# First product in blocks of 512 tokens, and the second weight's right half decoded after the attention

## Chip, core and metric

The kernel runs on one NeuronCore of one Trainium2 chip. The metric is the device time of the whole program in microseconds (us). The core has five engines with their own instruction streams, each in order: PE (matrix products; weights go in through PEld beside it), DVE (elementwise work and reductions), ACT (copies with rounding, exp, Mish), POOL (elementwise work without access to PSUM) and SP (issues the DMAs here).

## The reference

```python
# q, k, v: (8 batches, 8 heads, 576 positions, 64)
scores = scale * np.matmul(q, k.transpose(0, 1, 3, 2))
thresh = np.max(scores, axis=-1, keepdims=True) - tau
scores = np.where(scores >= thresh, scores, -1000000000.0)
attn = np.exp(scores - np.max(scores, axis=-1, keepdims=True))
attn = attn / (np.sum(attn, axis=-1, keepdims=True) + 1e-09)
x = np.matmul(attn, v)      # heads side by side: 4608 tokens x 512
h = x @ w_in                # 512 x 2048
g = h * np.tanh(sp)         # sp = log(1 + exp(h)): Mish
out = g @ w_out             # 2048 x 512
```

The two weights arrive as 64-bit floating point numbers and are turned into 32-bit ones in the kernel ("decoded").

## The kernel before

**Precision.** PE works on `fp32r` operands, which keep fewer bits than a 32-bit number. So a number is split into a rounded upper part (a cast on ACT) and a remainder (a subtraction on DVE or POOL), and a product is made of three matmuls: upper by upper, upper by lower, lower by upper. `xh`, `xl` are the parts of x, `w1h`, `w1l` those of w_in; `hi`, `lo` those of the transposed weights of attention.

**Attention.** 288 tiles (32 pairs of heads, nine tiles each), counted by g, in a loop of steps. A step works on several tiles at different stages: `scores` (PE) of tile g+1 into one of two PSUM tiles `s0`, `s1`; `row_max` (DVE) of tile g, its exponentials (ACT, tile `e`) and `masked` (DVE, `p`); `normalise` of g-1 (POOL); `transposes` of g-2 (PE, `tp`, one PSUM buffer); `evacuate_hi` (ACT) and `lo_main` (DVE) of g-3, which read `tp`; and the products with the values of older tiles (`y`). Every engine runs in the order in which the step's code is written.

**First product.** Between the steps of batch b runs `gemm1` of batch b-1, a generator that yields after each matmul. `advance` draws a number of matmuls per step, from the tables `MIX`, `MIX_FIRST` and `MIX_LAST`; `DRAIN` is the number in the five steps after the last tile. `gemm1` makes, for each half of 288 tokens of the batch (`HB`) and each of the 16 blocks f of 128 rows of h, 12 matmuls into a PSUM tile (4 blocks of the model dimension by the three kinds), a copy by ACT into `hst`, and after two blocks a store to DRAM (`hd`).

**Decoding.** A piece is 128 x 256 numbers, loaded as pairs of 32-bit words. `first` scales both words (two activations on ACT), `clamp`, `shift` and `sign` run on DVE, `add` on POOL. In the attention the loop spreads these over several steps. w_in comes first. Then, every 14th step (`W2_STEP`), comes one of the 16 pieces of w_out's right half (`decode_w2`, tile `dec`), which goes back to DRAM (`w2d`). In the attention's last steps five pieces of the left half are decoded (`decode_top`) and four more loaded.

**Last stage of the first product.** The last batch's `gemm1` runs after the attention, in 32 units of 12 matmuls. Ahead of each unit stand the works that the table `todo` has for it: pieces of w_out's left half, and the operands of the second product. In this stage a PSUM tile is taken from `psh` (three buffers) where f % 5 is below 3, and from `psx` (two buffers, named `hx`) otherwise.

**Second product.** Strassen's method with seven products for each pair of 512 tokens by blocks of 256. It needs w_out's blocks a11, a12 (left half), a21, a22 (right half), and the sums s1 = a21 + a22, r21 = a11 - a21, r22 = a22 - r21, r12 = a12 - r22 (split as s4), each a tile of 8 x 256 columns that is split in an upper and a lower part. `combine` makes a sum in two halves of 1024 columns on DVE. `load_raw` reads a block of h, `mish` applies the function, `operand` splits it into four `ring` tiles of two rows each. The nine pairs run in order of tokens. A pair of 512 tokens does not match a batch of 576, so `load_h` reads from up to two half-batch tensors.

`units` hands out places for 8 x 256 tiles, `home()` places for pieces.

Of the kernel before, what the change touches and what calls it, by code (L numbers as in the profile page):

```python
# [5 lines left out]
F32 = mybir.dt.float32  # L6
# [8 lines left out]
P = 128  # L15
# [4 lines left out]
W2_STEP = 14  # L20
STAGES = ((0, 1, 1), (0, 1, 1), (0, 2, 4))
THIRD = ((),)
LAG = 2
XSPLIT = (4, 1, 2)
# [13 lines left out]
NBLK = 2 * B  # L38
TC = 256
G = 2  # L40
# [27 lines left out]
MIX = (11, 12, 6, 9, 8, 13, 12, 14, 16, 6, 16, 4, 12, 4, 15, 5, 16, 13)  # L68
MIX_FIRST = (11, 12, 6, 9, 8, 13, 6, 14, 22, 6, 16, 4, 12, 4, 15, 9, 16, 13, 7, 12, 5, 10, 8, 13, 12, 14, 16, 6, 16, 4, 12, 4, 15, 5, 16, 13)
MIX_LAST = (12, 14, 16, 6, 16, 4, 12, 4, 15, 5, 16, 13, 11, 12, 6, 9, 8, 13, 12, 14, 16, 6, 16, 4, 12, 4, 15, 5, 16, 13, 11, 12, 6, 9, 8, 13)  # L70
DRAIN = 18
# [115 lines left out]
def attention_moe(tc, q, k, v, tau, w_in, w_out, out):  # L187
# [3 lines left out]
    with ExitStack() as outer:  # L191
# [11 lines left out]
        with ExitStack() as first:  # L203
# [21 lines left out]
            with ExitStack() as att:  # L225
# [64 lines left out]

                def decode_w2(f):
                    st = home()
                    work = Decode(nc, st, None, None)
                    work.load(w_out[f * P:(f + 1) * P, WC:])

                    def last():
                        nc.sync.dma_start(w2d[:, f], fv(work.a))

                    return [(work.first, skip), *spread(work, STAGES[2]), (last,)]

# [234 lines left out]
                def split_x(g, x):  # L535
                    parts = []
                    for c in range(2):
                        xh = xpool.tile([P, HB], F32R, name="xh", bufs=12)
                        xl = xpool.tile([P, HB], F32R, name="xl", bufs=12)
                        parts.append((xh, xl))  # L540

                    def half(c):
                        xh, xl = parts[c]
                        sl = slice(c * HB, (c + 1) * HB)
                        nc.scalar.copy(xh, x[:, sl])
                        (nc.vector if g >= NT else nc.gpsimd).tensor_tensor(xl, x[:, sl], fv(xh), ALU.subtract)
# [3 lines left out]
                    return parts  # L550

                def gemm1(b, xs):

                    halves = (range(NF // 2), range(NF // 2, NF))
                    if b < B - 1:
                        order = [(c, fs) for c in range(2) for fs in halves]
                    else:
                        order = [(c, fs) for fs in halves for c in range(2)]
                    for c, fs in order:
                        for f in fs:  # L560
                            if b < B - 1 or f % 5 < 3:
                                h = psh.tile([P, 512], F32, name="h", tag="ph")
                            else:
                                h = psx.tile([P, 512], F32, name="hx")
                            half, at = divmod(f * P, DF // 2)
                            i = 0
                            for d in range(ND):
                                xh, xl = xs[d][c]
                                wh, wl = (w[:, d, at:at + P] for w in w1[half])
                                for a, m in ((wh, xh), (wh, xl), (wl, xh)):  # L570
                                    nc.tensor.matmul(h[:, :HB], a, m, start=i == 0, stop=i == 3 * ND - 1)
                                    i += 1
                                    if i < 3 * ND:
                                        yield
                            if f % 2 == 0:
                                hst = xpool.tile([P, 2, HB], F32, name="hst", bufs=3)
                            nc.scalar.copy(hst[:, f % 2], h[:, :HB])
                            if f % 2 == 1:
                                nc.sync.dma_start(hd[2 * b + c][:, f - 1:f + 1, :], hst)
                            yield  # L580
# [8 lines left out]
                weights2 = [lambda f=f: decode_w2(f) for f in range(NF)]  # L589
# [35 lines left out]
                def close_pair(g, pi):  # L625
                    b, hp = divmod(pi, NP)
                    batches.setdefault(b, []).append(split_x(g, pairs.pop(pi)["x"]))
# [17 lines left out]
                for g in range(NT + 5):  # L645
# [96 lines left out]
                    if b >= 1:  # L742
                        if step == 0:
                            stream = gemm1(b - 1, batches.pop(b - 1))
# [18 lines left out]

            def load_h(to, fs, at, end):

                start = at
                while at < end:
                    i, off = divmod(at, HB)
                    m = min(HB - off, end - at)
                    nc.sync.dma_start(to[:, :, at - start:at - start + m], hd[i][:, fs, off:off + m])  # L770
                    at += m
# [16 lines left out]
            def load_raw(blk, pair):  # L788

                fh, th = blk  # L790
                raw = units.take(F32)
                at = (2 * pair + th) * TC
                for s in halves:
                    load_h(raw[:, s], slice(8 * fh + s.start, 8 * fh + s.stop), at, at + TC)
                return raw
# [18 lines left out]
            homes = [(t, t[:, 4 * i:4 * i + 4].rearrange("p a b -> p (a b)")) for t in homes for i in range(2)]  # L814

            def fetch_piece(n, st):
                f = PIECE[n]
                work = Decode(nc, st, None, None, (r12 if f >= 8 else r11)[:, f % 8])
                work.load(w_out[f * P:(f + 1) * P, :WC])
                return work  # L820

            coming = early_pieces
            for work, f in zip(coming, PIECE[5:]):
                if f < 8:
                    work.to = r11[:, f].bitcast(U32)
            for n in range(9, 10):
                coming.append(fetch_piece(n, home()))
            for n in range(10, 14):
                coming.append(fetch_piece(n, homes[n - 10][1]))
            r21, r22, s1 = (units.take(F32) for _ in range(3))  # L830
            for _ in stream:
                pass
            stream = gemm1(B - 1, batches[B - 1])
            a12, a12u, a12d = split(r12)
            b21 = None
            todo = {}

            def at(u, *works):
                todo.setdefault(u, []).extend(works)

            def piece(n):
# [6 lines left out]
            for n in range(5, 16):  # L848
                at(n - 5, lambda n=n: coming[n - 5].first())
                at(n - 4, lambda n=n: piece(n))  # L850
            for i in range(2):
                at(i, lambda i=i: coming.append(fetch_piece(14 + i, home())))

            state = {}
# [5 lines left out]
            def sum1():  # L860
                run_all(combine(s1, r21, r22, ALU.add))

            def split_into(name, raw):
                def go():
                    state[name], ups, downs = split(raw() if callable(raw) else raw)
                    run_all(ups)
                    run_all(downs)
                return go

            at(3, *a12u)  # L870
            at(12, *a12d)
            at(13, sum1)
            at(14, split_into("s1", s1), lambda: units.give(s1))
            at(15, lambda: state.update(b21=load_raw((1, 0), 0)))
            at(3, lambda: nc.sync.dma_start(r21, w2d[:, :8]))
            at(4, lambda: nc.sync.dma_start(r22, w2d[:, 8:]))
            at(7, lambda: state.update(b12=load_raw((0, 1), 0)))
            at(12, lambda: [units.give(t) for t in {id(t): t for t, _ in homes}.values()])
            at(16, lambda: mish(state["b12"]))
            at(15, split_into("a11", r11))  # L880
            at(17, lambda: run_all(combine(r21, r11, r21, ALU.subtract)), lambda: units.give(r11),
               lambda: state.update(b11=load_raw((0, 0), 0)))
            at(19, split_into("a22", r22))
# [201 lines left out]
```

## Time and profile before

Three runs took 1307.69 to 1309.09 us, with a median of 1308.76.

| | us |
|---|---|
| median of three runs | 1308.76 |
| the profiled execution | 1309.47 |
| its span, first to last instruction | 1307.7 |
| attention, first to last row maximum | 6.8 to 892.7 |
| first product of the last batch, first to last matmul | 908.2 to 960.3 |
| second product | 960.3 to 1307.7 |

The span holds what the engines' instructions cover; the rest of the execution's time lies around it. The clock that PE was granted is 0.997 of the full one over the span, so it does not enter. Matmuls overlap in the profile: one lasts some 290 ns there, while the next starts after 110 to 150. The price of a matmul is therefore the distance from start to start, which is the length of a dense stretch divided by its count.

### The profile page before, as it was taken

The numbers are of one execution on the slowest core, as the hardware profiler recorded it, in microseconds if no ns is written. First come the engines' busy times: TensorE is split into PE (matmuls) and PEld (weight loads), VectorE is DVE, ScalarE is ACT, GpSimd is POOL, SyncE is SP. The second block draws the span as 40 slices with busy tenths as digits, with TensorE's granted clock in tenths as the row PEclk, the third lists the DMA queues.
The fourth block names the chain that finished last, engine by engine and source line by source line (L and its number), as shares of the span: only waits on it lengthen the run. The fifth ranks groups of instructions, "written<-read, shape, count | busy, mean of one in ns | idle before, by whom it ended". The sixth has DMA issues, their size and how long they took to land.

```text
span 1307.7 us, 30494 instructions
## 1 busy us (share of the span) xinstructions
PE 1277.3 (98%) x9875; PEld 1235.7 (94%) x9875; DVE 1143.1 (87%) x2947; ACT 1031.8 (79%) x2320; POOL 747.9 (57%) x1080
## 2 busy tenths in 40 slices
PE   8998899999999999999999999999999999999998
PEld 7766889999999999999999999999999999999998
DVE  7999999999999999999999999998888777887774
ACT  5888888888888888888888888877778676666663
POOL 4778888888788888888888788874200000000000
PEclk9999999999999999999999999999999999999999
DMA  5335544444444444445444444433845545543540
GB/s 186 116 104 138 152 134 148 130 138 132 131 141 130 149 140 126 144 127 154 127 123 148 130 145 135 136 99 103 290 122 153 142 134 161 162 130 107 137 129 33
DMA packets 171982, 178.69 MB, mean 137 GB/s; under 512 B 46640, under 2 KB 139824, under 8 KB 171568
## 3 DMA queue, kind: packets, MB, share of 16 engines
q1 hardware_dynamic: 171680, 176.61, 45.7%
q8 instruction: 79, 1.29, 0.4%
q14 instruction: 79, 0.65, 0.2%
q10 hardware_dynamic: 144, 0.13, 0.0%
HBM read 109.05 MB, written 49.28 MB: 121 GB/s over the span
## 4 chain that ended last, share of the span: by engine, by line
PE 70%; DVE 17%; ACT 8%; issue 4%; POOL 1%; DMA 0%; ACTq 0%; DVEq 0%; POOLq 0%
PE h L95 21%; PE y L95 15%; PE x L95 10%; PE s L95 8%; PE z L95 7%; DVE st L95 6%; PE tp L95 6%; DVE p L95 4%; ACT e L95 3%; PE hx L95 3%; DVE dec L95 2%; DVE lo L95 2%; DVE tk L95 1%; ACT hi L95 1%; ACT k L95 1%
## 5 line engine op out<-in xcount | busy, mean ns | idle before, releaser
L95 PE MATMUL h<-xh,w1h 128*128 128x288 f32 x976 | 295.1, 302 | 2.6 <-ACT yo L95 1.1
L95 PE MATMUL h<-xh,w1l 128*128 128x288 f32 x976 | 292.3, 299 | 0.0
L95 PE MATMUL h<-xl,w1h 128*128 128x288 f32 x976 | 288.3, 295 | 0.3 <-DVE xl L95 0.3
L95 POOL TENSOR_SCALAR p<-p,st 128x576 f32<-128x576 f32 x288 | 242.1, 841 | 65.0 <-DVE st L95 40.2
L95 ACT ACTIVATE e<-s,st 128x580 f32<-128x580 f32 x288 | 215.3, 748 | 63.7 <-DVE st L95 56.9
L95 DVE SCALAR_TENSOR_TENSOR p<-s,st,e 128x580 f32<-128x580 f32 x288 | 236.4, 821 | 19.1 <-ACT e L95 7.3
L95 DVE TENSOR_REDUCE st<-s 128x1 f32<-128x580 f32 x288 | 218.0, 757 | 1.1 <-PE s L95 0.3
L95 PE MATMUL s<-k,q 128*128 128x290 f32 (+1 forms) x1056 | 197.0, 310 | 9.0 <-DVE p L95 7.8
L95 DVE TENSOR_TENSOR ring<-un,ring 128x512 fp32r<-128x512 f32 x252 | 157.3, 690 | 48.5 <-ACT ring L95 45.1
L95 DVE TENSOR_TENSOR lo<-tp,hi 128x512 fp32r<-128x512 f32 (+1 forms) x280 | 173.3, 627 | 25.1 <-ACT hi L95 22.9
L95 PEld LDWEIGHTS h<-xh,w1h 128*128 128x128 f32 x976 | 184.1, 189 | 6.8 <-ACT yo L95 4.1
L95 PEld LDWEIGHTS h<-xl,w1h 128*128 128x128 f32 x976 | 183.9, 188 | 0.5 <-DVE xl L95 0.5
L95 PE MATMUL tp<-ident,p 128*128 128x128 f32 x1152 | 174.3, 274 | 10.0 <-DVE lo L95 5.5
L95 PEld LDWEIGHTS h<-xh,w1l 128*128 128x128 f32 x976 | 183.7, 188 | 0.0
L95 PEld LDWEIGHTS s<-k,q 128*128 128x128 f32 x1056 | 158.0, 190 | 22.5 <-DVE p L95 19.3
L95 ACT CAST hi<-tp 128x512 fp32r<-128x512 f32 (+1 forms) x280 | 150.2, 547 | 35.5 <-PE tp L95 31.6
L95 ACT CAST ring<-un 128x512 fp32r<-128x512 f32 x252 | 138.9, 619 | 39.5 <-DVE un L95 36.3
L95 PEld LDWEIGHTS tp<-ident,p 128*128 128x128 f32 x1152 | 137.9, 140 | 22.1 <-POOL k L95 7.0
L95 PE MATMUL y<-hi,vs 128*128 128x256 f32 (+1 forms) x448 | 132.0, 317 | 3.0 <-ACT hst L95 2.4
L95 PE MATMUL x<-ring,un 128*128 128x256 f32 x1152 | 134.6, 276 | 0.0
L95 PEld LDWEIGHTS x<-ring,un 128*128 128x128 f32 x1152 | 132.4, 188 | 0.2 <-issue 0.2
L95 PE MATMUL y<-lo,vs 128*128 128x256 f32 (+1 forms) x448 | 121.8, 295 | 0.0
(94 smaller groups left out, 2602.1 us busy)
## 6 DMA issues: line engine op xcount, KB each, us to landing
hd<-hst SPq DMA_DIRECT2D x128, 288.0 KB, 2.6
r<-q SPq DMA_DIRECT2D x120, 160.0 KB, 2.5
r<-k SPq DMA_DIRECT2D x120, 160.0 KB, 2.2
r<-v SPq DMA_DIRECT2D x56, 160.0 KB, 2.4
dec<-w_in SPq DMA_DIRECT2D x32, 256.0 KB, 2.9
un<-hd SPq DMA_DIRECT2D x16, 512.0 KB, 5.2
kph<-k SPq DMA_DIRECT2D x56, 144.0 KB, 3.0
kpl<-k SPq DMA_DIRECT2D x56, 144.0 KB, 3.0
```

The costliest lines, as they stand in the source:

```text
L95: made = method(*args, **kwargs)
```

## The change

1. **Blocks.** The first product works on blocks of 512 tokens: the first 512 tokens of each batch, and a ninth block of the last 64 tokens of all eight. A block and f take 12 matmuls of 512 columns, one copy by ACT and one store. `hd` has nine tensors, one a block. The tables' numbers of matmuls are about half of those before.
2. **Tails.** `split_x` also stores the last 64 columns of x of each pair of heads to `xd`. After the attention the four tensors are loaded into the unit `rest` and split in units 1 to 4. The ninth block runs in the last stage beside the last batch: eight f of the one, eight of the other, and so again, 32 units of 12 matmuls as before.
3. **The right half of w_out** is decoded in the last stage: 27 pieces there (four left, 16 right, seven left), two in each unit, where there were 11, one a unit. `decode_w2`, `w2d` and its stages are gone. A later piece's load stands behind the `add` of the piece nine before it, whose place it takes.
4. **Pairs are blocks**: the second product's pairs read one tensor each. The tails' block comes last but one, and its results are stored in pieces of 64 columns. b21 of the first pair is dropped after its split and loaded again for the second product.

The places at which the order of instructions matters are these three. In each row stands the line of the helper, the operation, what is written and what is read (with the tile's number), and the columns.

PE in the attention, around the transposes of one tile; s1 is the scores' PSUM tile, h the first product's. Before:

```order
L95 MATMUL s1_141<-k20_7150,q0_7148 128x286
L95 MATMUL h_7655<-xl_7463,w1h_96 128x288
L95 MATMUL h_7655<-xh_7462,w1l_97 128x288
L95 MATMUL h_7705<-xh_6053,w1h_96 128x288
L95 MATMUL h_7705<-xl_6054,w1h_96 128x288
L95 MATMUL h_7705<-xh_6053,w1l_97 128x288
L95 MATMUL h_7705<-xh_6513,w1h_96 128x288
L95 MATMUL h_7705<-xl_6514,w1h_96 128x288
L95 MATMUL h_7705<-xh_6513,w1l_97 128x288
L95 MATMUL tp_7712<-ident_80,p_7579 128x128 x4
```

Now, at the same tile:

```order
L95 MATMUL s1_137<-k20_6455,q0_6453 128x286
L95 MATMUL h_6886<-xh_5898,w1l_93 128x512
L95 MATMUL h_6886<-xh_6324,w1h_92 128x512
L95 MATMUL h_6886<-xl_6325,w1h_92 128x512
L95 MATMUL h_6886<-xh_6324,w1l_93 128x512
L95 MATMUL tp_6931<-ident_76,p_6826 128x128 x4
```

Eight matmuls of 288 columns between the scores and the next tile's transposes became four of 512.

SP at the start of the last stage; `un` and `dec` are places for pieces, `un_13248` the unit `rest`, hd the stores of h. Before:

```order
L131 DMA dec_14993<-w_out 128x512
L131 DMA un_14991<-w_out 128x512 x2
L131 DMA un_14992<-w_out 128x512 x2
L131 DMA dec_15006<-w_out 128x512
L131 DMA dec_15029<-w_out 128x512
L579 DMA hd14_78<-hst_15021 128x576
```

Now:

```order
L131 DMA dec_13249<-w_out 128x512
L131 DMA un_13243<-w_out 128x512 x2
L131 DMA un_13244<-w_out 128x512 x2
L845 DMA un_13248<-xd0_63 128x512
L845 DMA un_13248<-xd1_64 128x512
L845 DMA un_13248<-xd2_65 128x512
L845 DMA un_13248<-xd3_66 128x512
L562 DMA hd7_74<-hst_13286 128x512
```

The four loads of the tails stand behind the same five loads of pieces, where the next two pieces' loads stood.

ACT in the last stage, units 19 to 23; `un_13850` is the upper part of s4, `un_13726` the block b21, hx a PSUM tile of `psx`. Before (`un_107` is r12, `un_15470` the upper part of s4, `un_15318` b21):

```order
L95 COPY hst_15468<-hx_15455 128x288
L95 CAST un_15470<-un_107 128x1024 x2
L95 COPY hst_15468<-h_15476 128x288
L95 COPY hst_15509<-hx_15496 128x288
L95 CAST ring_15511<-un_15318 128x512
```

Now:

```order
L95 COPY hst_13827<-h_13814 128x512
L95 ACTIVATE un_13726<-un_13726 128x1024 x2
L95 COPY hst_13847<-h_13834 128x512
L95 CAST un_13850<-un_103 128x1024 x2
L95 COPY hst_13869<-hx_13856 128x512
L95 COPY hst_13885<-hx_13872 128x512
L95 CAST ring_13888<-un_13726 128x512
```

The casts of s4 stand ahead of the evictions of units 21 and 22 now, which hold the two buffers of `psx`; they stood ahead of unit 23's before.

The diff, cut to its core:

```diff
-XSPLIT = (4, 1, 2)
+XSPLIT = (4, 1, 1)
-MIX = (11, 12, 6, 9, 8, 13, 12, 14, 16, 6, 16, 4, 12, 4, 15, 5, 16, 13)
+MIX = (6, 6, 3, 4, 4, 7, 6, 7, 8, 3, 8, 2, 6, 2, 7, 3, 8, 6)
...
-DRAIN = 18
+DRAIN = 9
...
-        w2d = dram.tile([P, NF, WC], F32, name="w2d")
-        hd = [dram.tile([P, NF, HB], F32, name=f"hd{i}") for i in range(NBLK)]
+        xd = [dram.tile([P, B * TL], F32, name=f"xd{d}") for d in range(ND)]
+        hd = [dram.tile([P, NF, TM], F32, name=f"hd{i}") for i in range(B + 1)]
...
+                def gemm1(chunks):
+
+                    parts = (range(NF),) if len(chunks) == 1 else (range(NF // 2), range(NF // 2, NF))
+                    for to, xs, f in [(to, xs, f) for fs in parts for to, xs in chunks for f in fs]:
+                        if len(chunks) == 1 or f % 5 < 3:
+                            h = psh.tile([P, 512], F32, name="h", tag="ph")
+                        else:
+                            h = psx.tile([P, 512], F32, name="hx")
...
+                                nc.tensor.matmul(h, a, m, start=i == 0, stop=i == 3 * ND - 1)
...
+                        hst = xpool.tile([P, TM], F32, name="hst", bufs=2)
+                        nc.scalar.copy(hst, h)
+                        nc.sync.dma_start(to[:, f], hst)
...
-                    elif not weights and weights2 and g % W2_STEP == 0:
-                        decoding.append([()] * LAG + weights2.pop(0)())
...
+            wanted = [(PIECE[n], 0) for n in range(5, 9)]
+            wanted += [(f, 1) for f in range(NF)]
+            wanted += [(PIECE[n], 0) for n in range(9, NF)]
...
             def piece(n):
-                work = coming[n - 5]
+                work = coming[n]
                 work.clamp()
                 work.shift()
                 work.sign()
                 work.add()
+                if n + 9 < len(wanted):
+                    fetch(n + 9)
...
+            def split_rest(d):
+                xh, xl = rest_x[d]
+                nc.scalar.copy(xh, left[:, d])
+                nc.vector.tensor_tensor(xl, left[:, d], fv(xh), ALU.subtract)
...
+            for d in range(ND):
+                at(d + 1, lambda d=d: split_rest(d))
+            at(5, lambda: units.give(rest))
+            for n in range(len(wanted)):
+                at(n // 2, lambda n=n: coming[n].first())
+                at(n // 2 + 1, lambda n=n: piece(n))
+            at(3, *a12u)
+            at(12, sums(s1, r21, r22, ALU.add))
+            at(13, split_into("s1", s1), lambda: units.give(s1))
+            at(14, fetch_h("b12", (0, 1)))
+            at(15, lambda: [units.give(t) for t in homes], split_into("a11", r11), fetch_h("b21", (1, 0)))
+            at(16, *a12d, sums(r21, r11, r21, ALU.subtract), lambda: units.give(r11))
+            at(17, fetch_h("b11", (0, 0)))
+            at(18, split_into("a22", r22), spread_mish("b12"))
+            at(19, sums(r22, r22, r21, ALU.subtract))
+            at(20, sums(r12, r12, r22, ALU.subtract), spread_mish("b21"))
+            at(21, split_into("s4", r12), lambda: units.give(r12))
...
+        sequence = [*range(B - 1), B, B - 1]
```

More of the change, by code (lines that the diff above doesn't have):

```diff
@@ L533, in values, with operands_x @@
                     return gather
[L535 to L540, printed above, removed]
-                    def half(c):
[L543 to L546, printed above, removed]
+                def operands_x():
+                    return [xpool.tile([P, TM], F32R, name=f"x{n}", bufs=2 * ND) for n in "hl"]
@@ L549, in split_x @@
                     chores.setdefault(g + XSPLIT[1] + XSPLIT[2], []).append(lambda: half(1))
[L550 to L580, printed above, removed]
@@ L826, in attention_moe @@
[L826 to L830, printed above, removed]
+            r21, r22, s1, rest = (units.take(F32) for _ in range(4))
+            slots = [t[:, 4 * i:4 * i + 4].rearrange("p a b -> p (a b)") for t in homes for i in range(2)]
+            wanted = [(PIECE[n], 0) for n in range(5, 9)]
+            wanted += [(f, 1) for f in range(NF)]
@@ new lines, in attention_moe, with fetch @@
+            wanted += [(PIECE[n], 0) for n in range(9, NF)]
+            coming = early_pieces
+            for work, (f, _) in zip(coming, wanted):
+                work.to = (r12 if f >= 8 else r11)[:, f % 8].bitcast(U32)
+            def fetch(n):
+                f, right = wanted[n]
+                to = ((r11, r12), (r21, r22))[right][f // 8][:, f % 8]
+                work = Decode(nc, home() if n % 9 < 5 else slots[n % 9 - 5], None, None, to)
+                work.load(w_out[f * P:(f + 1) * P, right * WC:(right + 1) * WC])
+                coming.append(work)
@@ L846, in piece @@
                 work.add()
[L848 to L854, printed above, removed]
-            def run_all(works):
-                for w in works:
-                    w()
-            def sum1():
-                run_all(combine(s1, r21, r22, ALU.add))
+                if n + 9 < len(wanted):
+                    fetch(n + 9)
             def split_into(name, raw):
                 def go():
-                    state[name], ups, downs = split(raw() if callable(raw) else raw)
+                    state[name], ups, downs = split(raw)
                     run_all(ups)
@@ L868, in split_into, with sums, fetch_h, spread_mish @@
                 return go
[L870 to L883, printed above, removed]
[L884 to L887 removed]
+            def sums(to, x, y, op):
+                return lambda: run_all(combine(to, x, y, op))
+            def fetch_h(name, blk):
+                return lambda: state.update({name: load_raw(blk, 0)})
+            def spread_mish(name):
+                return lambda: mish(state[name])
+            left = rest.rearrange("p (d c) t -> p d (c t)", c=2)
+            for d in range(ND):
+                nc.sync.dma_start(left[:, d], xd[d])
+            def split_rest(d):
+                xh, xl = rest_x[d]
+                nc.scalar.copy(xh, left[:, d])
+                nc.vector.tensor_tensor(xl, left[:, d], fv(xh), ALU.subtract)
             def first_t1():
@@ L911, in attention_moe @@
         wf.tile([P, 16], F32, name="pad")
-        units.add(wl, 2)
+        units.add(wl, 3)
         ring.add(wg, 8)
```

143 lines of the change are left out of this document (78 added, 65 removed).

## The prediction

> **What bounds the kernel now.** First the page: its span and the busy time of each engine.
>
> ```profile
> span 1307.7 us, 30494 instructions
> PE 1277.3 (98%) x9875; PEld 1235.7 (94%) x9875; DVE 1143.1 (87%) x2947; ACT 1031.8 (79%) x2320; POOL 747.9 (57%) x1080
> ```
>
> PE looks like the bound throughout, but overlapping matmuls hide short waits in that number, and the stages differ. So the next view is the busy time by stage: three stretches of the attention, its drain, the last batch's first product (from its first matmul at 908.2), the second product (from 960.3). Columns: stretch, length, busy time and instruction count of each engine.
>
> ```profile
> 176.20:231.20 55.00, 52.94 (x403) 51.38 (x404) 51.69 (x154) 46.74 (x114) 47.05 (x70) 1.00 0.46 137
> 231.20:785.70 554.50, 549.24 (x4212) 539.56 (x4211) 518.76 (x1520) 480.76 (x1167) 465.83 (x693) 1.00 0.46 136
> 785.70:892.70 107.00, 106.36 (x825) 105.28 (x824) 99.92 (x296) 90.91 (x220) 83.92 (x128) 1.00 0.38 113
> 892.70:908.20 15.50, 15.32 (x117) 14.91 (x116) 10.88 (x30) 11.46 (x30) 6.75 (x11) 1.00 0.28 94
> 908.20:960.30 52.10, 51.23 (x385) 50.78 (x384) 45.05 (x64) 39.87 (x80) 10.30 (x13) 1.00 0.77 252
> 960.30:1307.70 347.40, 343.60 (x3027) 343.24 (x3025) 257.14 (x361) 220.86 (x354) 0.00 (x0) 1.00 0.45 127
> ```
>
> In the attention DVE (third pair) is busy 51.69+518.76+99.92 = 670.4 of 716.5 us. What are the missing 46 us? The waits, from 176 to 893 us, by who waited for whom (total, times, longest):
>
> ```profile
> DVE lo L95 <- ACT hi L95: 18.4, 46, 0.6
> ```
>
> Only 18.4 us are waits that the view can name; ACT's `hi` copies the transposes, so this is DVE waiting for PE through ACT. The other 28 us are pieces of a tenth of a microsecond between dependent instructions, which stay. So attention has two bounds at once: PE, and 3% behind it DVE. Whatever takes load off PE gains only until DVE's own row is full.
>
> **The price of a matmul.** First a dense stretch of 288-column matmuls, then one of 256 columns, then the first and last of seven with 320 (start, duration).
>
> ```profile
> 920.00:950.00 30.00, 30.00 (x228) 30.00 (x227) 27.00 (x33) 20.80 (x39) 5.66 (x7) 1.00 0.79 267
> 1100.00:1200.00 100.00, 100.00 (x885) 100.00 (x884) 73.28 (x101) 64.92 (x103) 0.00 (x0) 1.00 0.47 129
> ```
> ```profile
> 509.57 0.31 PE L95 MATMUL y<-hi,vs 128*128 128x320 f32 x1
> ...
> 510.45 0.31 PE L95 MATMUL y<-tk,vs 128*128 128x320 f32 x1
> ```
>
> Start to start: 30.0/228 = 131.6 ns for 288, 100/885 = 113.0 for 256, 0.88/6 = 147 for 320. No row has 512. Twice the 256 gives 226 ns; going on from 288 at the slope to 320 (0.48 ns a column) gives 239. I take 226, since 512 is two full 256s, and keep 216 to 239: no row excludes that a long matmul is a little cheaper, so 10 ns below stay open. The first product then falls from 3072 x 131.6 = 404 us of PE to 1728 x 226 = 391: of this 2688 x 131.6 - 1344 x 226 = 50 us leave the attention, and the last stage grows from 384 x 131.6 = 50.5 to 384 x 226 = 86.8, by 36.3.
> The Trainium skill's page "TensorE: Matmul & The Clock Gate", section "Back-to-back issue gap", gives N/2.4 + 2.5 ns; that is 122.5 for 288, where the trace has 131.6, so the trace does not bear it out, and 215.8 for 512. By it merging would save only the 2.5 ns of 1344 matmuls, 3.4 us; with that price for the new matmuls the sum below would be 1 us lower.
>
> **Attention: minus 39 us.** (1) The second weight's right half is no longer decoded here. Its instructions, by the tile `dec` (DVE, ACT, POOL):
>
> ```profile
> 176.20:880.00 703.80, 24.97 (x49) 12.60 (x33) 13.39 (x18) 1.00 0.45 134
> ```
>
> 16 of these 17 pieces go: 24.97 x 16/17 = 23.5 us of DVE, on the bound, so all of it counts. Two neighbouring pairs of heads, with and without (all instructions, then `dec` alone), say the same:
>
> ```profile
> 397.92:426.30 28.38, 28.26 (x220) 27.93 (x218) 26.38 (x80) 24.67 (x61) 22.90 (x36) 1.00 0.41 119
> 426.30:452.30 26.00, 26.00 (x205) 25.98 (x204) 24.66 (x73) 23.38 (x57) 23.56 (x35) 1.00 0.52 157
> ```
> ```profile
> 426.40:452.40 26.00, 0.10 (x1) 0.77 (x2) 0.75 (x1) 1.00 0.52 157
> 397.90:426.40 28.50, 1.26 (x3) 0.77 (x2) 0.00 (x0) 1.00 0.41 120
> ```
>
> (2) PE has 50 us less, over twice what DVE loses, so PE now runs ahead and the `lo` waits mostly go. Bounds: none of the 18.4 us, or all. I take three quarters, 13.8, because some steps still hold a value product beside the first product. (3) Five drain steps are PE's alone: 18 x 131.6 - 9 x 226 ns = 0.33 us each, 1.7 in all. Sum 23.5 + 13.8 + 1.7 = 39.0; bounds 23.5 to 44. PE cannot gain its whole 50: DVE is late next.
> At nothing: 32 stores of the 64-token tails (32 KB, DMA busy 0.46 of the time), splits of 256 in place of 288 columns (POOL, 84% busy), and the evictions, by these rows of groups (count, busy, mean; `ysb` is a copy of 512 columns), 16 of 590 ns a batch against 32 of 401, which lightens ACT.
>
> ```profile
> L95 ACT COPY hst<-h 128x288 f32<-128x288 f32 x244 | 95.0, 401 | 29.8 <-PE h L95 26.2 <-DMA hd<-hst 2.3
> ...
> L95 ACT COPY ysb<-y 128x512 f32<-128x512 f32 x9 | 5.3, 590 | 14.3 <-PE y L95 14.3
> ```
>
> If ACT or POOL became late instead, it would show as `lo` waits, inside the bounds.
>
> **The last stage: plus 45 us.** Before, PE needs 50.5 and takes 52.1; the difference is the wait for the last pair's operands:
>
> ```profile
> 910.11 0.40 PE L95 MATMUL h<-xh,w1h 128*128 128x288 f32 x1 [0.58 <-ACT xh L95]
> 910.80 0.40 PE L95 MATMUL h<-xl,w1h 128*128 128x288 f32 x1 [0.29 <-DVE xl L95]
> ```
>
> If PE were fed, it would now take 1.1 + 86.8, and the stage would cost 36 us more. Whether it is fed hangs on DVE, which gets 27 pieces in place of 11, and four splits for the tails' block. I count from the stage's first matmul. SP's loads, before, and time to landing (KB, us):
>
> ```profile
> 911.80 1.80 SPq L131 DMA_DIRECT2D un<-w_out x4
> 913.70 1.69 SPq L131 DMA_DIRECT2D dec<-w_out x2
> ```
> ```profile
> dec<-w_out SPq DMA_DIRECT2D x5, 256.0 KB, 3.4
> ```
>
> The tails are loaded where the row of 913.70 stands, behind four pieces: issued at 5.5, landed at 8.9, copied by ACT at 9.5. DVE's first split stands ahead of piece 0, so DVE starts at 9.5. Then piece by piece (POOL's add of one beside DVE's clamp of the next), the 1024-column sums (ten in 12.37) and 512-column splits (four in 2.50):
>
> ```profile
> 919.34 1.11 DVE L95 TENSOR_SCALAR un<-un 128x256 f32<-128x256 f32 x2
> ...
> 920.49 0.43 DVE L95 SCALAR_TENSOR_TENSOR un<-un 128x256 uint32<-128x256 uint32 x1
> 920.83 1.12 DVE L95 TENSOR_SCALAR un<-un 128x256 f32<-128x256 f32 x2
> ...
> 921.05 0.75 POOL L95 TENSOR_TENSOR un<-un 128x256 uint32<-128x256 uint32 x1 [0.74 <-DVE un L95]
> ```
> ```profile
> 928.29 12.37 DVE L95 TENSOR_TENSOR un<-un 128x1024 fp32r<-128x1024 f32 x10
> 952.46 2.50 DVE L95 TENSOR_TENSOR ring<-un,ring 128x512 fp32r<-128x512 f32 x4
> ```
>
> A piece takes 920.83 - 919.34 = 1.49 us. Two a unit are 2.98 against PE's 12 x 0.226 = 2.71, so DVE falls behind by itself. Up to the sum into `r12` of unit 20, DVE does 4 x 0.62 = 2.5, 27 x 1.49 = 40.2, and 16 halves (sum and split for s1, split a11, a12's lower half, r21, split a22, r22, r12) x 1.237 = 19.8; at a11 it waits some 1.8 for POOL's add (0.75) and ACT's first half. That is 9.5 + 64.3 = 73.8.
> Who waits? ACT's casts of s4 stand ahead of unit 21's eviction and need that sum. Two such casts take ACT 2.01:
>
> ```profile
> 934.76 2.01 ACT L95 CAST un<-un 128x1024 fp32r<-128x1024 f32 x2
> ```
>
> The first can run while DVE sums the second half; the second ends at 74.8, and unit 21's eviction (0.59) at 75.4. Unit 24 (f = 8) needs that buffer: `psx` has two, which units 21 and 22 hold. PE would be there at 1.1 + 24 x 2.71 = 66.2, so it waits 9.2 us. Behind it stand only the last eight units: 75.4 + 8 x 2.71 = 97.1, against 52.1 before: **plus 45.0**. Earlier waits (unit 18 behind s1, unit 20 behind a11, each 2 to 4 us) are part of the 9.2, since the last one decides. SP also stops, at unit 17's load of b11 into r11's place until r21's sum, with evictions behind it; with two `hst` buffers that is felt at unit 19, whose buffer PE wants only in unit 26.
> Bounds: 36 (PE fed) to 50 (DVE 5 us later still, if landings are slower).
>
> **The second product** keeps its 3024 matmuls at 113 ns. b21 is loaded and put through Mish a second time (1 MB; ACT 2 us), and the tails' block is stored in 64-column pieces; ACT (220.86 of 347.40) and DMA (0.45) have room. Nothing.
>
> **Sum.** The profiled execution took 1309.47 (its span and 1.8 around it), 0.7 over the median of the runs. 1309.5 - 39.0 + 45.0 = 1315.5; less 0.7: **1315**.
>
> **Rivals.** (a) PE stays fed in the last stage. For it: five PSUM buffers let PE run some units ahead, and all of DVE's work fits into 97 us. Against it: the work stands ahead of an eviction that PE needs, in one row, with no gap to close. Price +36.3: 1306, and 1302 if all `lo` waits go too: faster. It decides if r12's sum comes before 64.6 (unit 24's 66.2 less 1.6), 9 us earlier than counted. Chance 0.18, half of it beyond 0.2%.
> (b) Attention gains the decode alone: `lo` waits stay because ACT or POOL, 87% and 84% busy, take PE's part. 1309.5 - 25.2 + 45 - 0.7 = 1329. Against it: ACT and POOL lose work as well. Chance 0.14.
> (c) The change is not what it says: a 512-column matmul costs 239. PE's attention then loses 32 us, still more than DVE; the last stage comes to 75.4 + 8 x 2.87 = 98.4. 1317. Chance 0.06.
> Forecast as counted, within some 7 us: 0.62.
>
> **How the numbers follow.** 0.2%, 2.6 us, is about what a measurement can tell here. Slower by more: (b), (c) and most of the forecast, 0.66. Within: the forecast's low end and half of (a), 0.20. Faster: the rest of (a) and a forecast where all waits go and the stall is short, 0.14. The range leaves out part of (b) above and the end of (a) below: 1304 to 1326.
>
> **What will show it.** Right: the attention's last row maximum at about 853 in place of 892.7, few `lo` waits; the last stage 97 long, DVE idle until 9 us into it, then full until 74; PE's `hx` waiting on ACT `hst` before unit 24, some 9 us with the earlier ones; 226 ns between 512-column matmuls. Wrong: no wait of `hx` there (a), or `lo` waits near 18 us (b).

## Result and the profile after

The changed kernel takes 1318.47 us in the median of six runs (1317.69 to 1319.23), the kernel before 1308.80 beside it. The ratio is 1.0074, with a 95% interval of 1.0061 to 1.0087: slower by 9.7 us. The forecast was 1315 in a range of 1304 to 1326, slower by more than 0.2%.

The page of the changed kernel begins so; PEclk is the granted clock in 40 slices, in tenths.

```profile
span 1316.3 us, 27626 instructions
...
PE 1275.5 (97%) x8531; PEld 1137.5 (86%) x8531; DVE 1140.1 (87%) x2951; ACT 1021.7 (78%) x2214; POOL 740.7 (56%) x1080
...
PEclk9999999999999999999999999998999999999999
```

PE's total busy time is nearly that of before (1277.3), so the page alone says little, but for one 8 in the clock: a slice that lies in the last stage. The busy times by stage (stretch, length, then busy time and count of PE, PEld, DVE, ACT, POOL, then granted clock, DMA share, GB/s) are those of the attention, its drain, the last stage, a piece of the last stage, and the second product:

```profile
176.20:851.60 675.40, 667.57 (x4194) 584.10 (x4195) 642.15 (x1913) 589.04 (x1364) 575.19 (x872) 1.00 0.44 127
...
851.60:865.60 14.00, 13.37 (x76) 11.21 (x75) 10.65 (x30) 10.68 (x26) 6.16 (x9) 1.00 0.30 98
...
865.65:968.90 103.25, 94.53 (x386) 74.76 (x385) 71.07 (x117) 58.70 (x116) 25.08 (x29) 0.95 0.61 196
894.00:900.00 6.00, 5.58 (x13) 4.42 (x14) 5.72 (x13) 3.50 (x10) 3.02 (x5) 0.50 0.73 225
...
968.90:1316.30 347.40, 343.59 (x3025) 343.35 (x3023) 256.42 (x360) 222.56 (x355) 0.00 (x0) 1.00 0.40 129
```

From 176.2 us to the last row maximum it is 675.4 us in place of 716.5, the drain 14.0 in place of 15.5, the last stage 103.2 in place of 52.1, the second product 347.4 as before. So the attention gave 42.6 us and the last stage took 51.1. The difference, 8.5, is the growth of the span (8.6).

**In the attention** DVE is busy 642.15 us in place of 670.37, 28.2 less; the `lo` waits fell:

```profile
DVE lo L95 <- ACT hi L95: 8.0, 30, 0.6
```

From 18.4 that is 10.4 less. 28.2 and 10.4, 2.5 of smaller gaps, and 1.5 of the drain make the 42.6. Of the 28.2, 24.97 are the `dec` row of the kernel before: in the changed kernel DVE has no such instruction in this stretch.

**In the last stage** PE waits twice and then runs at half speed. Timeline of PE (start, duration, in brackets the idle time and who ended it), around the wait before unit 8 and the one before unit 24:

```profile
884.63 0.40 PE L95 MATMUL h<-xl,w1h 128*128 128x512 f32 x1
...
889.06 0.39 PE L95 MATMUL h<-xh,w1l 128*128 128x512 f32 x1
894.42 0.79 PE L95 MATMUL h<-xh,w1h 128*128 128x512 f32 x1 [4.97 <-ACT hst L95]
...
895.44 0.63 PE L95 MATMUL h<-xh,w1l 128*128 128x512 f32 x1
...
899.71 0.63 PE L95 MATMUL h<-xh,w1h 128*128 128x512 f32 x1
```
```profile
945.12 0.79 PE L95 MATMUL hx<-xh,w1h 128*128 128x512 f32 x1 [3.00 <-ACT hst L95]
```

The first two rows are 20 matmuls, 19 steps: 4.43/19 = 233 ns start to start. The last two of the first fence are ten steps: 427 ns each, in the stretch where the granted clock is 0.50. Start to start, the two waits are 5.36 and 3.39 us, of which 0.23 each is the matmul's own.

Who is late? PE waits for ACT's evictions, so ACT's timeline comes next, ahead of unit 8 and of unit 24, with SP's queue ahead of unit 8:

```profile
877.19 0.62 ACT L95 CAST xh<-un 128x512 fp32r<-128x512 f32 x1 [6.71 <-DMA un<-xd]
...
893.78 0.59 ACT L95 COPY hst<-h 128x512 f32<-128x512 f32 x1 [4.07 <-DMA hd<-hst]
```
```profile
884.11 4.06 SPq L131 DMA_DIRECT2D dec<-w_out  x3
889.66 0.33 SPq L131 DMA_DIRECT2D un<-w_out  x1
890.08 0.86 SPq L562 DMA_DIRECT2D hd<-hst  x2
```
```profile
939.73 0.59 ACT L95 COPY hst<-h 128x512 f32<-128x512 f32 x1 [2.75 <-DMA hd<-hst]
940.21 2.01 ACT L95 ACTIVATE un<-un 128x1024 f32<-128x1024 f32 x2
942.12 0.57 ACT L95 COPY hst<-h 128x512 f32<-128x512 f32 x1
942.58 2.00 ACT L95 CAST un<-un 128x1024 fp32r<-128x1024 f32 x2
944.48 1.08 ACT L95 COPY hst<-hx 128x512 f32<-128x512 f32 x2
```

ACT stands still for 6.7 us for the tails' block, and for 4.1 us for a store of `hst` that SP issues only at 890.08, behind loads that themselves wait for a free place. Ahead of unit 24 stand another wait for a store, a Mish, and the casts of s4. These casts carry no idle time: they did not wait for r12's sum. The prediction said that they would. DVE's row says when that sum was there (the last two of these eleven), and SP's queue why the store was late:

```profile
927.83 12.58 DVE L95 TENSOR_TENSOR un<-un 128x1024 fp32r<-128x1024 f32 x11 [1.72 <-ACT un L95]
```
```profile
933.66 0.92 SPq L765 DMA_DIRECT2D un<-hd  x2
934.67 11.23 SPq L562 DMA_DIRECT2D hd<-hst  x6
```

The sum ends at 940.41, 2.1 us before the casts begin. The eviction at 939.73 is unit 19's; it needs the buffer of unit 17, whose store SP issues at 934.67, behind the two loads of b11. These wait for r21's sum, which ends at 933.6, five operations into the same DVE row.

The last stage is then: 384 x 233 ns = 89.5; 1.0 at the start; 5.1 and 3.2 of waits; and 4.4 for the half clock (17 matmuls at 427 ns, 3.3 over 233, and six in transition, some 1.1): 103.2. These terms say where PE's time went, not what each would save: a matmul that is cheaper ahead of a wait only makes the wait longer.

### The profile page after: what moved, and what is told of

It reads as the page before. It is cut to its first block, busy times and chain, and to the rows that moved or that the text cites. A ratio compares the mean times of both kernels' runs of the same rounds, so it can differ in the third digit from the quotient of the medians.

```text
span 1316.3 us, 27626 instructions
## 1 busy us (share of the span) xinstructions
PE 1275.5 (97%) x8531; PEld 1137.5 (86%) x8531; DVE 1140.1 (87%) x2951; ACT 1021.7 (78%) x2214; POOL 740.7 (56%) x1080
## 5 line engine op out<-in xcount | busy, mean ns | idle before, releaser
L95 PE MATMUL h<-xh,w1h 128*128 128x512 f32 x528 | 217.2, 411 | 5.9 <-ACT hst L95 5.0
L95 PE MATMUL h<-xl,w1h 128*128 128x512 f32 x528 | 213.9, 405 | 1.4 <-DVE xl L95 0.8
L95 PE MATMUL h<-xh,w1l 128*128 128x512 f32 x528 | 210.9, 399 | 0.0
L95 PEld LDWEIGHTS s<-k,q 128*128 128x128 f32 x1056 | 168.2, 189 | 41.4 <-DVE p L95 23.7
L95 DVE TENSOR_TENSOR un<-un 128x1024 f32<-128x1024 f32 (+1 forms) x94 | 110.8, 1235 | 9.2 <-ACT un L95 9.1
L95 PEld LDWEIGHTS h<-xh,w1h 128*128 128x128 f32 x528 | 100.3, 190 | 17.2 <-ACT hst L95 5.4
L95 PEld LDWEIGHTS h<-xh,w1l 128*128 128x128 f32 x528 | 100.3, 190 | 13.5
```

The lines of the kernel that those rows point to most:

```text
L95: made = method(*args, **kwargs)
```

## Experiments

The expectations call PE TensorE, DVE VectorE, ACT ScalarE, POOL GpSimd and SP SyncE. Below, "over before" is the time less that of the kernel before in the same group of runs; for the change it is 9.7. Stage is the time from the first matmul's start to the last's in the last stage: before 52.2, now 103.0. Of the last stage's waits those over 1.5 us are listed, start to start, with their unit. Where a run stands alone, differences of half a microsecond can't be told from none: the six runs of the changed kernel spread over 1.5 us.

| run | us (runs) | over before | stage | waits |
|---|---|---|---|---|
| w2_in_attention | 1332.60 (1) | 23.9 | 93.5 | 1.9 at 8 |
| short_xl | 1316.03 (1) | 7.8 | 105.0 | 5.6 at 8, 3.6 at 24 |
| rest_later | 1317.97 (1) | 9.2 | 102.3 | 2.2 at 20, 6.1 at 24 |
| stores_first | 1319.11 (1) | 10.4 | 104.2 | 5.3 at 8, 4.0 at 24 |
| both_moves | 1316.69 (4) | 8.0 | 101.5 | 2.1 at 20, 4.6 at 24 |
| late_s4 | 1317.36 (1) | 9.2 | 101.6 | 5.2 at 8, 3.3 at 24 |
| stores_act | 1318.24 (1) | 10.1 | 102.6 | 3.7 at 8, 4.1 at 24 |
| fed | 1310.42 (10) | 2.2 | 95.2 | 2.1 at 20, 2.3 at 24 |
| halves_only | 1317.39 (1) | 8.5 | 102.3 | 5.2 at 8, 1.6 at 23, 4.4 at 24 |
| a11_later | 1312.26 (7) | 3.4 | 95.7 | 3.6 at 24 |
| a11_later_halves | 1312.49 (6) | 3.6 | 97.9 | 4.9 at 24 |
| mish_later | 1306.18 (11) | -2.5 | 88.8 | none |

### What bounds the attention

Put back the right half's decode, and keep the blocks:

```diff
+                    elif not weights and weights2 and g % W2_STEP == 0:
+                        decoding.append([()] * LAG + weights2.pop(0)())
...
-            wanted += [(f, 1) for f in range(NF)]
```

> Blocks of 512 kept, but the right half of the second weight decoded in the attention as before the change, one piece every 14 steps, so 11 pieces in the last stage. If DVE's row is full in the attention: its 23.5 us of decoding come back one for one, the last row maximum moves from 852 to 873 to 877 us; the last stage, with DVE lightly loaded, has no wait and takes 91 to 92; the second product stays at 347: 1328 to 1331, slower than both kernels. If PE's new slack hides the decoding: the last row maximum stays below 860 and the time is 1307 to 1313.

Measured: 1332.60; last row maximum at 875.8, 24.2 us later than with the change. The attention's row:

```profile
225.00:875.80 650.80, 630.70 (x3904) 541.79 (x3904) 616.98 (x1822) 553.22 (x1295) 547.64 (x824) 1.00 0.45 131
```

DVE's busy time is 21.3 us more than over the same steps of the changed kernel (616.98 against 595.64 from 225 to 851.6), and the time 24.2 more. What DVE gets is paid in full. ACT gets 7.3 us more and POOL 15.5, too little each to explain the 24.2. (The last stage kept a wait of 1.9 us before unit 8 where none was expected and took 93.5 us, so the time lies 1.6 us above the expected range.) The other side, PE relieved and DVE not:

```diff
-                                nc.tensor.matmul(h, a, m, start=i == 0, stop=i == 3 * ND - 1)
+                                short = len(chunks) == 1 and m is xl
+                                to_ = h[:, :TC] if short else h
+                                nc.tensor.matmul(
+                                    to_, a, m[:, :TC] if short else m, start=i == 0, stop=i == 3 * ND - 1,
...
```

> The changed kernel with the xl by w1h matmuls of the first seven batches (32 a batch) on 256 of their 512 columns; the other 256 columns of that term are left out. This takes about 32 x (233 - 113) ns = 3.8 us, with both halves of the rows counted (64 such matmuls a batch) 7.7 us, of TensorE's work from each of seven batches and nothing from VectorE. Theory (in the attention the freed places were filled and VectorE's row now sets the pace: putting the decode back cost all its 23.5 us): the last row maximum stays within 4 us of 851.6, because TensorE only waits longer for VectorE. Rival (TensorE's own work sets the pace): the last row maximum falls by 25 to 54 us. The last stage and the second product stay.

Measured: last row maximum at 848.5, 3.0 us earlier. Its row, and that of the changed kernel for the same steps:

```profile
225.00:848.50 623.50, 602.11 (x3895) 518.42 (x3895) 594.37 (x1771) 540.39 (x1263) 531.29 (x807) 1.00 0.44 127
```
```profile
225.00:851.60 626.60, 619.61 (x3895) 542.61 (x3894) 595.64 (x1773) 545.94 (x1263) 532.16 (x807) 1.00 0.44 127
```

Six batches' products lie in this stretch, so some 46 us of PE's work were left out; its busy time falls by 17.5 (matmuls overlap there, which hides a part), the time by 3.0. The two runs together show that DVE, and no longer PE, sets the attention's pace in the changed kernel; in its row above DVE is busy for 95% of the stretch, ACT for 87% and POOL for 85%. No run loads DVE alone.

### What the last stage waits for: one thing at a time

The tails' splits two units later, so that DVE starts its pieces at once:

```diff
-                at(d + 1, lambda d=d: split_rest(d))
-            at(5, lambda: units.give(rest))
+                at(d + 3, lambda d=d: split_rest(d))
+            at(7, lambda: units.give(rest))
```

> The tails' four splits move from units 1 to 4 to units 3 to 6. If the late start of DVE (it idled 8.8 us until the tails had landed) is what PE's waits come from: DVE begins its pieces about 4 us into the last stage in place of 12, POOL's adds come 8 us earlier, PE's wait before unit 8 (5.1 us) goes and that before unit 24 (3.2) falls below 1, the clock stays full, the stage falls from 103 us to 91 to 92, the time to 1306 to 1308. If SP's order (loads that wait for POOL ahead of the stores) makes the wait at unit 8 whenever DVE starts: that wait stays at over 3 us, 1313 to 1315. If the sheer amount of DVE's work sets the stage: 1316 or more.

Measured: 1317.97. The wait before unit 8 goes (0.8 us are left inside that unit, for the tails' `xl`), but that before unit 24 grows to 6.1. ACT's and DVE's timelines of this run show why the early start was lost again:

```profile
880.45 0.59 ACT L95 COPY hst<-h 128x512 f32<-128x512 f32 x1 [4.99 <-DMA hd<-hst]
```
```profile
874.66 0.42 DVE L95 SCALAR_TENSOR_TENSOR dec<-dec 128x256 uint32<-128x256 uint32 x1
881.58 0.69 DVE L95 TENSOR_TENSOR xl<-un,xh 128x512 fp32r<-128x512 f32 x1 [6.50 <-DMA dec<-w_out]
```

ACT stops for a store, the tails' cast stands behind it, and DVE idles 6.5 us. (The view names a load; `xh` is written by ACT at 880.93, and that is what DVE's row reads.) DVE reaches r12's sum 72.5 us into the stage in place of 74.8. So the theory that DVE's late start was all was wrong. The number fits the third case, that the amount of DVE's work sets the stage; mish_later below rules that out. Next, the loads of later pieces behind the unit's store in SP's queue, alone and together with the move above:

```diff
-                    fetch(n + 9)
+                    queued.append(n + 9)
...
+                while queued:
+                    fetch(queued.pop(0))
```

> Each unit's loads of later pieces are issued behind the unit's store and not ahead of it; the tails' splits stay where they are. If the wait at unit 8 comes from stores that stand behind waiting loads, it goes with its slow clock (8 us less), but DVE starts as late as before, r12's sum still ends about 75 us into the stage, and PE, now early, waits 7 to 8 us before unit 24 in place of 3.2: 1314 to 1316. If the stores alone were the cause of all waits: 1306 to 1308. If ACT's late evictions at unit 8 have nothing to do with the stores: 1318 and the wait stays.

> Both moves together. If DVE's late start is the root of both waits, the second move adds nothing: within 1 us of the run with the splits moved alone, 1306 to 1308, and faster than the kernel before by 0.1 to 0.2%. If the two causes stand side by side, this run is 3 us or more below each of the two alone.

Measured: 1319.11 alone, with the wait before unit 8 unchanged (5.3). Moving the loads behind one store only puts them ahead of the next. Together with the tails' move 1316.69, ratio 1.0061 (1.0044 to 1.0078), 1.3 us below the one and 2.4 below the other alone: neither of the two cases expected. The step of the prediction itself, s4's casts ahead of the evictions, was tried by moving them:

```diff
-            at(21, split_into("s4", r12), lambda: units.give(r12))
+            at(25, split_into("s4", r12), lambda: units.give(r12))
```

> The changed kernel with one step moved: the split of s4 (two ScalarE casts of r12's sum) from unit 21 to unit 25. If these casts, waiting for r12's sum, hold up the evictions that unit 24 waits for (the step as the prediction had it), the wait before unit 24 (3.4 us) goes and with it the half clock behind it (some 1.2 us): 1313 to 1315. Rival: in the trace the casts follow a mish and an eviction that itself waited 2.75 us for the store of its hst buffer, so only the casts' own 1.9 us is won: 1316 to 1317.5.

Measured: 1317.36. The wait before unit 24 stays at 3.3, and only its end comes 1.7 us earlier (77.8 us into the stage). The rival held. Then the stores of h, out of SP's queue:

```diff
-                        nc.sync.dma_start(to[:, f], hst)
+                        (nc.sync if len(chunks) == 1 else nc.scalar).dma_start(to[:, f], hst)
```

> The changed kernel with the last stage's stores of h (32 DMAs) issued from ScalarE's queue, right behind the eviction that makes them, in place of SyncE's, where they stand behind loads that wait for a free slot or unit. If that place in SyncE's queue makes the evictions wait (ScalarE's eviction of unit 5 waits 4.07 us for the store of unit 3), the wait before unit 8 (5.4 us) and the half clock behind it (some 3 us) go; VectorE's pieces are no faster, so the wait before unit 24 may grow by up to what was won before it: 1312 to 1316. Rival (VectorE's and GpSimd's chain of pieces holds ScalarE's queue at unit 8): the wait stays above 4 us, 1318 to 1319.

Measured: 1318.24, no gain. Yet the waits of ACT for its stores up to 930 us fell from 10.1 us in 5 (the change) to these:

```profile
ACT hst L95 <- DMA hd<-hst: 0.6, 1, 0.6
```

ACT now issues each store itself (0.33 us and some 0.4 of idle time around it), and it still stands 7.2 us for the tails. After that it has no gap of a microsecond until 892, and unit 8 waits 3.7, which is 1.7 less. Unit 19's eviction no longer waits for a store either, yet unit 21's starts only 0.6 us earlier in the stage (78.3 in place of 78.8), and unit 24's wait is 4.1. The waits that were taken away were real, but ACT's other work ahead of the same evictions covered them. The time fits the rival (1318 to 1319), but not its mechanism: ACT did not wait for pieces there, it was late with its own work behind the stall for the tails.

### All at once

The tails' move, the stores on ACT, s4 at unit 25:

> All three moves together: the tails' split two units later, the stores of h on ScalarE's queue, s4's split at unit 25. If nothing but these holds TensorE up in the last stage, its waits fall below 3 us and its half clock goes, and the stage is 384 x 233 ns = 89.5 us, 1.5 us of start and up to 3 us of waits, 91 to 94 us: 1305 to 1309, about the kernel before. Rival (VectorE's serial work up to r12's sum, 72 us behind the stage's start, still holds units 20 to 24 back): 5 to 7 us of waits stay there: 1311 to 1314.

Measured: 1310.42, ratio 1.0019 (1.0010 to 1.0029), between the two theories. The stage is 95.2, no matmul runs at half clock, 4.4 us of waits are left (3.9 without the matmuls' own time). Alone, the three gained 0.5, 0.5 and -0.4 us against their own kernel before; together they gained 7.5. What is left of it begins in ACT's queue again:

```profile
923.08 1.04 ACT L95 CAST un<-un 128x1024 fp32r<-128x1024 f32 x1 [4.01 <-POOL un L95]
```

This is a11's second cast, which waits for the last piece, with evictions behind it. So it was moved, and a11's place given back, from units 15 and 16 to 18, a22's split from 18 to 19; and beside it each 512-column matmul was split into two of 256 columns, with and without these moves:

```diff
-            at(15, lambda: [units.give(t) for t in homes], split_into("a11", r11), fetch_h("b21", (1, 0)))
-            at(16, *a12d, sums(r21, r11, r21, ALU.subtract), lambda: units.give(r11))
+            at(15, lambda: [units.give(t) for t in homes], fetch_h("b21", (1, 0)))
+            at(16, *a12d, sums(r21, r11, r21, ALU.subtract))
...
+            at(18, split_into("a11", r11), lambda: units.give(r11))
```
```diff
+                                    for c in range(2):
+                                        sl = slice(c * TC, (c + 1) * TC)
+                                        nc.tensor.matmul(
+                                            h[:, sl], a, m[:, sl], start=i == 0 and c == 0, stop=i == 3 * ND - 1,
...
```

> The three moves together, and a11's split from unit 15 to unit 18 and a22's from 18 to 19. In the run with three moves one of a11's casts waits 4.01 us on ScalarE's queue for the last piece, and the evictions behind it come 2.1 us late for unit 20 and, with a table load and two mishes behind, 2.3 us late for unit 24. If ScalarE's order is all that is left, both waits go: 1310.4 less 4.4, 1305.5 to 1307. Rival (VectorE's chain holds what the mishes and casts wait for anyway): 1309 to 1311.

> The same, with each 512-column matmul of the last stage as two of 256 columns on the same weights. At 113 ns each in the attention's rows that is 226 ns in place of 233 to 235: 384 x 7 to 9 ns, 2.7 to 3.5 us less than the run before it, 1302 to 1304, if TensorE is fed and the pair costs what single ones did. Rival: a second load of the weights shows, 256 columns give no more than 512: 0 to 4 us more than the run before it.

> The changed kernel with only this halving in the last stage. The waits before units 8 and 24 end when ScalarE's evictions come, whatever TensorE's price; what it gains ahead of them is waited for, and only the eight units behind the wait before unit 24 keep it: 96 x 7 to 9 ns, 0.7 to 0.9 us: 1317 to 1318. Rival (the waits follow TensorE's own pace): the full 2.7 to 3.5 us: 1315 to 1316.

Measured: 1312.26 (ratio 1.0026, 1.0015 to 1.0036) and 1312.49 (1.0030, 1.0018 to 1.0042): no gain from either, and a11_later lies above both of its expected ranges. Unit 20's wait went, and unit 24's grew. In ACT's timeline of a11_later, ahead of unit 24 (PE resumes at 937.91):

```profile
928.15 2.00 ACT L95 CAST un<-un 128x1024 fp32r<-128x1024 f32 x2 [1.42 <-DVE un L95]
930.17 1.28 ACT L95 ACT_TABLE_LOAD   x1
931.46 2.01 ACT L95 ACTIVATE un<-un 128x1024 f32<-128x1024 f32 x2
933.38 0.57 ACT L95 COPY hst<-h 128x512 f32<-128x512 f32 x1
...
934.35 2.00 ACT L95 ACTIVATE un<-un 128x1024 f32<-128x1024 f32 x2 [0.40 <-ACT hst L95]
936.26 0.56 ACT L95 COPY hst<-h 128x512 f32<-128x512 f32 x1
...
937.27 0.59 ACT L95 COPY hst<-hx 128x512 f32<-128x512 f32 x1 [0.45 <-ACT hst L95]
```

From 928.15 to 936.26 ACT has work with hardly a pause, and 7.3 of these 8.1 us are a22's casts, a table load and two Mishes for the second product; the evictions stand behind them. The halved matmuls cost 113 to 114 ns, so PE is faster, but it then waits 4.9 us. Alone they gave 1.2 of the 9.7 us, as expected of a stage that ACT paces: 1317.39.

The last run keeps the halves and all the moves, and puts that work behind the evictions. DVE's last two sums move with it, in the same order, to unit 21:

```diff
-            at(19, split_into("a22", r22), spread_mish("b12"))
-            at(19, sums(r22, r22, r21, ALU.subtract))
-            at(20, sums(r12, r12, r22, ALU.subtract), spread_mish("b21"))
-            at(25, split_into("s4", r12), lambda: units.give(r12))
-            at(23, first_operand, spread_mish("b11"))
...
+            at(21, split_into("a22", r22), sums(r22, r22, r21, ALU.subtract), sums(r12, r12, r22, ALU.subtract))
+            at(23, spread_mish("b12"))
+            at(24, spread_mish("b21"))
+            at(25, first_operand, fetch_h("b22", (1, 1)))
+            at(26, split_into("s4", r12), lambda: units.give(r12))
+            at(27, spread_mish("b11"))
...
```

> As the run with a11's split later and halved matmuls, with a22's split at unit 21 and ScalarE's mishes of the coming blocks (2.0 us each, the first with a table load of 1.28 us) at 23, 24, 27 and 28 in place of 19, 20, 23 and 26. In that run they stand before the evictions that unit 24 waits 4.9 us for. If the order of ScalarE's work is what feeds or starves TensorE, the wait before unit 24 falls below 1 us, no matmul goes at half clock, the last stage is 768 x 114 ns = 87.6 us and up to 3 us more, 89 to 91 us, and the time 1303 to 1306, below the kernel before (1308.8). Rival (VectorE's chain or the stores of h hold the evictions all the same): 3 to 5 us of waits stay, at unit 24 or a later one: 1309 to 1313.

Measured: 1306.18, ratio 0.9985 (0.9976 to 0.9994): faster than both kernels, than the one before by 0.15% (the forecast took 0.2% as what can be told from no change). Its rows for the last stage, a piece of it, and the start of the second product:

```profile
865.64:954.50 88.86, 88.24 (x770) 87.43 (x769) 70.70 (x117) 59.93 (x115) 24.93 (x29) 1.00 0.68 223
905.00:935.00 30.00, 29.88 (x263) 29.68 (x262) 26.75 (x37) 16.24 (x26) 8.84 (x9) 1.00 0.68 229
```
```profile
954.50:975.00 20.50, 17.46 (x146) 16.86 (x144) 12.38 (x17) 13.89 (x24) 0.00 (x0) 1.00 0.42 139
```

The stage is 88.9 at full clock with no wait of a microsecond, though DVE still ends the sum into r12 late:

```profile
931.08 6.90 DVE L95 TENSOR_TENSOR un<-un 128x1024 fp32r<-128x1024 f32 x6 [2.73 <-ACT un L95]
```

That is 72.3 us into the stage, 5.2 us after unit 24 began. The time is 0.2 above the expected range. In the profiled execution, which at 1308.31 us is 2.1 above the median, 4.4 us came back in the second product (954.5 to 1306.3, 351.8 us against 347.4): PE waits there for operands whose casts stand behind the stage's last eviction,

```profile
959.84 0.58 ACT L95 COPY hst<-h 128x512 f32<-128x512 f32 x1 [4.20 <-DMA hd<-hst]
```

which again waits for a store to leave its `hst` buffer free. A version without this was not tried.

## Why the prediction came out as it did

The sign and the time held (1315 against 1318.47, inside the range). The two terms were 42.6 against 39.0 and 51.1 against 45.0. The errors, 3.6 and 6.1 us, partly cancelled; that the total came so close is in part luck. They leave 2.5 of the 3.5 us. The other 1.0 is that the profiled execution was 0.3 below the median here, and 0.7 above it before.

- **Attention, the bound.** Right: DVE's row is full, PE's further gain is lost. Shown by w2_in_attention and short_xl.
- **Attention, the size.** DVE's busy time fell by 28.2 for 23.5. The prediction took 16/17 of the `dec` row's 24.97 us, for 16 of 17 pieces; but its 49 instructions are 16 pieces of three and one more, and all of it went. The `lo` waits gave 10.4, not 13.8; the drain 1.5 for 1.7. That the view's waits name only part of what a relieved PE gives back (2.5 us came from smaller gaps) was left out of the sum. Rival (b), that these waits stay near 18 us, is ruled out by the 8.0.
- **Price of 512 columns.** 233 ns, not 226; it lies between the choice and rival (c)'s 239. 384 x 7 ns is 2.7 us of PE's time in the stage, but ahead of a wait it costs nothing: only the 96 matmuls behind unit 24 pay it, 0.7 us, and halves_only won 1.2 and not 2.7. Two matmuls of 256 columns do cost 226 to 228, as the last runs show. The formula of the Trainium skill's page "TensorE: Matmul & The Clock Gate", section "Back-to-back issue gap", 215.8, which that section gives for isolated matmuls, is not borne out at 512 either.
- **Waits of PE.** 8.3 us for a predicted 9.2 after the start, but not as predicted: 5.1 before unit 8, which the prediction did not have, and 3.2 before unit 24.
- **The step that failed** is "ACT's casts of s4 stand ahead of unit 21's eviction and need that sum", with DVE's chain of 64.3 us as the gate. The chain ended nearly on time (r12's sum 74.8 us into the stage; predicted 73.8), if by two errors: it began at 12.2 in place of 9.5 and took 62.6. But it was not the gate: the casts began 2.1 us after it, moving them left the wait, and in mish_later, with the casts at unit 26, PE does not wait though the sum ends after unit 24 has begun. By the sum alone unit 21's eviction would have ended at some 942.0 (an estimate: 940.41, a cast of 1.0, a copy of 0.59), 3 us before it did. What gates PE is the order of work on ACT: evictions behind casts, Mishes and the tails' splits that come early, and behind stores that SP holds back. The prediction saw SP's stop at unit 17, and that unit 19's eviction would feel it, but took it for harmless because PE wants that buffer only in unit 26. ACT works in order, though: that eviction waited 2.75 us, and a Mish, the casts and unit 21's eviction stood behind it.
- **A term was missing**: the half clock behind a long wait, 4.4 us in all. In the prediction's own terms the 6.1 us are, to 0.1, these: unit 24 begins at 79.5 in place of 75.4 (4.1), its last eight units cost 0.7 more by the price, and some 1.4 for the half clock behind that wait. What the slow matmuls behind unit 8 added stands ahead of unit 24's wait, and no run shows that it lengthened the stage.
- **Rival (a)**, PE stays fed, was counted out because DVE's row has no gap to close. The runs show that it can be had with DVE's row as full as it is: in mish_later the stage is 36.8 us longer than before, for the rival's 36.3, with ACT's work in another order and halved matmuls. The sign by which the prediction would have known it, r12's sum before 64.6, did not appear there (72.3) and was not needed.
- **Second product**: nothing, as predicted (347.4 and 347.4).

## What to carry to other kernels

Where an engine that works in order both frees buffers for the bound engine and prepares later work, list its queue unit by unit, with every store and load that it waits for; the arithmetic of the slowest chain alone does not say who waits. When one wait is covered by another, single edits show nothing (here 0.5, 0.5 and -0.4 us) and only all together do (7.5), so a failed single edit doesn't clear its cause. Work that is moved off a full engine adds no waits to the stage that takes it only if that stage keeps its evictions ahead of it.

## What the runs showed of the hardware

A wait of PE can cost more than its length. In the last stage of these kernels each wait of 3.25 us or more (start to start) was followed by 5 to 13 matmuls of 512 columns at 427 ns in place of 233, 1 to 2.5 us more, or, with halved matmuls, by some at 213 ns in place of 113; after waits up to 2.3 us none was slow. The number does not follow the wait's length: 5 after 5.17 us in late_s4, 13 after 3.60 us in short_xl. The Trainium skill's page "TensorE: Matmul & The Clock Gate", section "Part 1: The HAM clock gate", gives half the clock after an idle window of about 3.4 us; the traces agree roughly, with slow matmuls already after 3.25 us in late_s4, of which PE was idle for 2.85.

The price of a column is not the same for all lengths: 113 ns for 256, 131.6 for 288 and 233 for 512 columns, so two matmuls of 256 columns take 5 to 7 ns less than one of 512 (2 x 113 in the second product, 2 x 114 in mish_later's last stage).
